# Relu-squared attention and a gated FFN on one core: first loads split, output blocks interleaved, a new rule for bursts in the planner

## The chip, the cores and the metric

The kernel runs on one core of one Trainium2 chip. Its time is the device time in microseconds (us). The engines are named as in the profile: PE (TensorE, matmul), PEld (its weight loads), DVE (VectorE), ACT (ScalarE), POOL (GpSimd, which issues the input loads), SP (SyncE, which issues the output stores and the DMA transposes).

## The reference

For 8 batches of 12 heads, 448 positions and head size 64, scores = q kT / 8, attention = relu(scores)^2 / 448, times v. The heads are laid side by side as x (3584 tokens by 768), and the FFN is (relu(x Wg) * (x Wv)) Wout with d_ff 1536:

```
scores = scale * np.matmul(q, k.transpose(0, 1, 3, 2))
attn = np.maximum(scores, 0.0) ** 2 / S
x = matmul(attn, v)  # heads side by side
gate = np.maximum(x @ w_gate, 0.0)
return (gate * (x @ w_val) @ w_out).astype(np.float32)
```

Inputs and output are fp32 in HBM; the kernel computes in bf16 with fp32 sums.

## The kernel before, in words

**Work.** A quad is four heads of one batch: 3 quads per batch, 24 in all. For each quad q and k are brought into the layout qkT (head dimension on partitions), for batches 0 and 1 by PE transposes (`transpose_pe`, L384; copies out of PSUM by L406 on ACT or L408 on DVE), later by a DVE permutation (L428) and a DMA transpose that SP issues (L434). `Attention.s(i)` (L470) is one of seven score steps of a quad: four 64x64 matmuls that run side by side (L478) into a pair of PSUM banks, a relu (L488 on ACT or L490 on DVE), and a square (L499 or L501). `Attention.pv` (L508) multiplies the seven squared blocks with v (28 matmuls, L516), and L531 or L533 copies the result to xT. Batch 0 is done in two parts: query columns 0 to 191 of all three quads, then 192 to 447.

**FFN.** Batches 0 and 1 use `gv_plain` (L556, matmuls L568): 12 blocks of 128 columns of d_ff, each a gate product and a value product of six matmuls. The first six blocks of batch 0 are done for its two parts separately. Later pairs of batches use `gv_strassen` (L633, matmuls L668): seven products of three matmuls per block, named p1 to p7, in which sums accumulate in the same PSUM bank and are copied out between them (`snapshot`, L625, ACT L617/L619 or DVE L621/L623; L687, L698, L709, L725 on DVE). So p5 waits for the copy after p6, and p3 for the addition (v1, L687) after p5. The output product of each pair of batches is `out_tail` (the 128 odd rows, four products) and then `out_strassen` (three blocks i of seven products, matmuls L769): in a block the order is p1, p7, p6, p4, p5, p2, p3, with `evac_add` (L759, DVE) after p4, p5 (called o22) and p2, and p3 waiting for o22. The four sums `sh` (L806, DVE) that feed a block wait for all of h (the hidden values) of the pair.

**Order.** All five engines' orders are written when the kernel is built, by `plan` (L128): a greedy list planner with modelled costs per operation and engine, which commits at each step the operation that can start first. Operations of ACT and DVE (`others`) go to whichever engine ends them first. POOL's loads go in the order in which they are declared (`pool`), with at most eight on their way. PE draws from three lists: `first` (transposes, scores and PVs of batch 0, part one), then `att` (the rest of attention) and `ffn`, each in its own fixed order. Scores come in bursts of two. A new burst starts when the FFN time since the last one (`since`) has reached `gap` (the FFN work left in the segment, over the bursts left until its deadline) and attention can start at most 0.15 us after the FFN operation:

```
if att[ai][1] == last_burst:
    pick = "A" if A[0] <= F[0] + 0.4 else "F"
elif since >= gap:
    pick = "A" if A[0] <= F[0] + 0.15 else "F"
else:
    pick = "F" if F[0] <= A[0] + 0.3 else "A"
```

**Buffers.** PSUM has eight banks. Attention uses pairs of banks (0,1) and (2,3) (`PAIRS`; four pairs for batch 0, `FIRST_PAIRS`); FFN products use the single banks 7, 6, 5, 4 (`SINGLES`). There are ten buffers for squared scores (`at`), three for qkT, one for the hidden values hT.

**Loads.** At the start POOL issues k and q of the three quads of batch 0 (L364, L365), with the making of the identity matrix (for PE's transposes) after the first two of them, then v, then the weights in six chunks of 256 columns (L334, gate and value of each), with the quads of batch 1 between: chunks 0, 1, quad a, chunk 2, quads b and c, chunks 3, 4, 5.

Of the kernel before, what the change touches and what calls it, by code (L numbers as in the profile page):

```python
# [22 lines left out]
class Buf:  # L23
# [7 lines left out]
    def pick(self):  # L31
        best = None
        for i in self.among:
            if all(i + w in self.res.free for w in range(self.width)):
                t = max(self.res.free[i + w] for w in range(self.width))
                if best is None or t < best[0]:
                    best = (t, i)
        return best
# [16 lines left out]
class Planner:  # L55
# [5 lines left out]
    RESERVE = 16  # L61
# [7 lines left out]

    def ready(self, op):  # L70
        r = 0.0
        for d in op.deps:
            if d.end is None:
                return None
            r = max(r, d.end + (self.LATE if d.xbar else 0.0))
        for b in op.alloc:
            p = b.pick()
            if p is None:
                return None
            r = max(r, p[0])  # L80
        return r
# [17 lines left out]
    def commit(self, op, s, e):  # L99
        op.start, op.eng = s, e  # L100
        occ, busy = op.engs[e]
        self.t[e] = s + occ
# [11 lines left out]
        for b in op.alloc:  # L114
            b.idx = b.pick()[1]
# [12 lines left out]
def plan(first, att, ffn, others, pool, deadline):  # L128
# [3 lines left out]
    P = Planner()  # L132
    ai = fi = pi = 0
# [5 lines left out]
    active = [o for o in others if not o.missing]  # L139
    def done(op):  # L140
# [5 lines left out]
    last_burst = last_grp = None  # L146
    since = gap = 0.0
# [3 lines left out]

    first = [list(x) for x in first]
    while any(first) or ai < len(att) or fi < len(ffn) or active or pi < len(pool):
# [5 lines left out]
        if pi < len(pool):  # L159
            b = P.best(pool[pi])  # L160
            if b is not None:
# [3 lines left out]
                cands.append((s, 0.0, 0, "POOL", pool[pi]))  # L165
        if any(first):
# [4 lines left out]
            s, _, kind, e, op = min(cands, key=lambda c: c[:3])  # L171
            P.commit(op, s, e)
            done(op)
            if kind == 0:
                pi += 1
            elif kind == 1:
                active.remove(op)
            else:
                first = [x[1:] if x and x[0] is op else x for x in first]
            continue  # L180
        A = P.best(att[ai][0]) if ai < len(att) else None
        F = P.best(ffn[fi][0]) if fi < len(ffn) else None
        pick = None
        if ai < len(att) and fi < len(ffn) and last_grp is not None and last_grp == ffn[fi][0].grp:
            pick = "F" if F is not None else None
        elif A is not None and F is not None:
            if att[ai][1] == last_burst:
                pick = "A" if A[0] <= F[0] + 0.4 else "F"
            elif since >= gap:
                pick = "A" if A[0] <= F[0] + 0.15 else "F"  # L190
            else:
                pick = "F" if F[0] <= A[0] + 0.3 else "A"
        elif A is not None:
            pick = "A"
        elif F is not None:
            pick = "F"
        if pick == "A":
            cands.append((A[0], A[2], 2, "PE", att[ai][0]))
        elif pick == "F":
            cands.append((F[0], F[2], 2, "PE", ffn[fi][0]))  # L200
        assert cands, f"no operation can start: {ai} {fi} {len(active)} {pi}"
# [5 lines left out]
        elif kind == 1:  # L207
            active.remove(op)
        elif pick == "A":
            if att[ai][1] != last_burst:  # L210
                last_burst = att[ai][1]
                since = max(0.0, since - gap)
            ai += 1
            last_grp = None
            sg = ffn[fi][1] if fi < len(ffn) else None
            left = deadline(sg) - last_burst + 1 if sg is not None and deadline(sg) is not None else 0
            gap = max(0.0, left_work[sg] - (P.RESERVE if sg == 0 else 0.0)) / max(1, left) if left > 0 else 0.0
        else:
            since += op.engs["PE"][0]
            left_work[ffn[fi][1]] -= op.engs["PE"][0]  # L220
            last_grp = op.grp
            fi += 1
# [5 lines left out]
def kernel(  # L228
# [31 lines left out]
    HALF = 3 * P2  # L260
# [34 lines left out]
    r_raw, r_perm, r_vv, r_qt, r_at = Res(N_RAW), Res(N_PERM), Res(N_VV), Res(N_QT), Res(N_AT)  # L295
# [13 lines left out]
    PAIRS, FIRST_PAIRS = [0, 2], [0, 2, 4, 6]  # L309
# [47 lines left out]
    def load_qk(b, g):  # L357
# [5 lines left out]
        src = lambda x: x[b, hs].rearrange("h (p t) d -> p h t d", t=NT)  # L363
        k_op = dma_in(lambda: st.raw()[64:128], src(k), 256, 1.15, alloc=[] if early else [st.raw_buf])  # L364
        q_op = dma_in(lambda: st.raw()[0:64], src(q), 256, 1.15)  # L365
# [17 lines left out]

    def transpose_pe(b, g):  # L384
        st = quads[(b, g)]
        ps2 = bank2(FIRST_PAIRS if b == 0 else PAIRS)

        def emit():
            raw = st.raw()
            for j in range(2):  # L390
                for t in range(NT):
                    for h2 in range(2):
                        nc.tensor.transpose(ps_b[64 * h2:64 * h2 + 64, ps2.idx + j, t * 128:(t + 1) * 128],
                                            raw[:, 2 * j + h2, t, :], ident)

        st.qt_buf = Buf(r_qt)
        op = pe(emit, 1.05, deps=st.qk_ops + [id_op], alloc=[ps2, st.qt_buf])
        st.qt_ops = []
        for j in range(2):
            cp = Op({"DVE": (0.6, 0.72), "ACT": (0.8, 0.95)}, None, deps=[op], reads=[ps2])  # L400

            def emit_cp(cp=cp, j=j):
                dst = qkT_t[st.qt_buf.idx][:, :, j, :].rearrange("p a (t c) -> p t a c", c=P2)
                src = ps_b[:, ps2.idx + j, :NT * 128].rearrange("p (t a c) -> p t a c", t=NT, a=2)
                if cp.eng == "ACT":
                    nc.scalar.copy(dst, src)  # L406
                else:
                    nc.vector.tensor_copy(dst, src)  # L408

            cp.emit = emit_cp  # L410
            st.qt_ops.append(cp)
            others.append(cp)
        return op

    def transpose_dma(b, g):
# [24 lines left out]
        st.qt_ops = [op]  # L440
# [11 lines left out]
    class Attention:  # L452
# [7 lines left out]
        def at_of(self, i):  # L460
            flat = at_t[self.at[i].idx].rearrange("p h c -> p (h c)")
            return flat[:, :2 * self.n].rearrange("p (h c) -> p h c", h=2)
# [7 lines left out]
        def s(self, i):  # L470
            ps2 = bank2(self.pairs)
            n = self.n
            at = self.at[i] = Buf(r_at)
# [7 lines left out]
            op = pe(emit, mm_time(1, n) + 0.01, deps=self.st.qt_ops, alloc=[ps2, at], reads=[self.st.qt_buf],  # L481
# [60 lines left out]
    hbuf, h_ops = {}, {}  # L542
# [5 lines left out]
    def pair_h(b):  # L548
        pr = b // 2
        if pr not in hbuf:  # L550
            hbuf[pr] = Buf(r_h)
            h_ops[pr] = []
            return [hbuf[pr]]
        return []

    def gv_plain(b, seg, blocks=range(KF), c0=0, n=S):  # L556
        cols = slice(c0, c0 + n)
        x_ops = xop[b] if b in xop else [o for c in xparts if n == S or c == c0 for o in xop[(b, c)]]
        for mf in blocks:
# [3 lines left out]
            for w, w_op in ((wg, wg_op), (wv, wv_op)):  # L563
# [16 lines left out]
                deps=[ops[1], grel], alloc=pair_h(b), reads=[bufs[1], gb])  # L580
            h_ops[b // 2].append(vmul)
# [51 lines left out]
    def gv_strassen(b, seg, T_ops):  # L633
# [44 lines left out]
        for mf in range(KF + 1):  # L678
# [5 lines left out]
            if prev is not None:  # L684
# [8 lines left out]
                    deps=[v1, prev["g1"]], reads=[vb, prev["g1b"]])  # L693
                others.append(h1)

            def p3_of(prev, v1, h1):
# [3 lines left out]
                    deps=[p3, prev["g0"]], reads=[prev["A"], prev["g0b"]], alloc=pair_h(b))  # L700
                h_ops[b // 2].extend([h0, h1])
                h1.deps.append(h0)
                others.append(h0)

            if cur is not None:
# [12 lines left out]
                if prev is not None:  # L718
                    p2_of()
                    p3_of(prev, v1, h1)  # L720
# [8 lines left out]
            else:  # L729
                p3_of(prev, v1, h1)  # L730
# [45 lines left out]
    def out_tail(b, seg, T_ops):  # L776
# [3 lines left out]
        lhs = lambda par: lambda kf: hT[:, 2 * kf + par, S - P2:S + P2]  # L780
        w = lambda par, hf: lambda kf: wo[:, par, hf, kf, :]
        h_lo = h_ops[pr][:-2]
        A, Bk = bank(), bank()
        wd = list(wo_op.values())
        slots = ((b, NT - 1), (b + 1, 0))
# [169 lines left out]
```

## Time and profile before

| | us |
|---|---|
| device time, median of 6 runs | 424.49 (423.62 to 427.26) |
| device time of the profiled execution | 424.81 |
| its span, first to last instruction | 422.9 |
| PE busy | 397.0 (94%) |
| DVE busy | 314.5 (74%) |
| ACT busy | 270.1 (64%) |
| POOL busy | 72.5 (17%) |

The granted clock of PE is 0.998 over the span. Of the chain of work that ended last, PE has 77%, DMA 9%, ACT 5%, DVE 4%. The loads of the inputs run until about 60 us at some 200 GB/s, and then one quad at a time beside the attention. The last PE matmul starts at 417.1 us.

A row of the order of time is: start, duration, engine, line, operation, what it writes and reads, how many merged; in brackets the engine's idle time before it and what ended that. A busy PE is not PE at its peak: the ends of matmuls are modelled, so gaps below some 0.2 us do not show as idle, and PE's own pace has to be taken from stretches in which nothing lies between the matmuls.

### The profile page before, as it was taken

To read this page: it belongs to the slowest core of one execution; us is meant where nothing else is said; L and a number is where in the kernel's file an instruction comes from. 1 tells how busy PE (TensorE), PEld (TensorE's weight loads), DVE (VectorE), ACT (ScalarE), POOL (GpSimd) and SP (SyncE) were. 2 spreads that over 40 slices of the span, in tenths; PEclk is the share of its full clock that TensorE was granted. 3 is DMA by queue.
4 is the path that set the end of the run, shared out by engine and by line. 5 is a ranking of instruction groups with operands and counts; after the bars stand their busy time and mean duration, and the time that the engine had idled before them with its cause. 6 is when DMAs were issued, how large, how long until landed. Compare 5 with 4: busy or idle time off the path is not lost.

```text
span 422.9 us, 8622 instructions
## 1 busy us (share of the span) xinstructions
PE 397.0 (94%) x3396; PEld 206.3 (49%) x3396; DVE 314.5 (74%) x569; ACT 270.1 (64%) x411; POOL 72.5 (17%) x118
## 2 busy tenths in 40 slices
PE   2878998999999999999999999999999999999994
PEld 2666653444444444444445554444455555554552
DVE  1785666997888989897788668998987647667451
ACT  3886886877778977877685556766767543343221
POOL 7746231122212211222120012021000000000000
PEclk9999999999999999999999999999999999999999
DMA  8999999997788998987737687354002430000144
GB/s 121 191 200 200 199 164 181 100 110 110 77 134 147 171 173 110 111 98 87 110 45 122 149 166 104 50 79 65 2 2 67 115 81 2 1 2 0 39 117 108
DMA packets 74920, 43.42 MB, mean 103 GB/s; under 512 B 36992, under 2 KB 74880, under 8 KB 74880
## 3 DMA queue, kind: packets, MB, share of 16 engines
q0 software_dynamic: 32512, 23.60, 41.3%
q1 hardware_dynamic: 42368, 19.28, 26.8%
q8 instruction: 26, 0.43, 0.4%
q14 instruction: 14, 0.11, 0.1%
HBM read 47.19 MB, written 11.01 MB: 138 GB/s over the span
## 4 chain that ended last, share of the span: by engine, by line
PE 77%; DMA 9%; ACT 5%; DVE 4%; issue 2%; POOL 1%; SPq 0%; DVEq 0%; POOLq 0%
PE ps L668 33%; PE ps L769 20%; PE ps L568 10%; PE ps L478 7%; PE ps L516 7%; DMA wv<-in_moe_w_val_dram 4%; DMA qkT<-perm 3%; ACT at L488 3%; DMA gvT<-in_k_dram 2%; DVE at L490 2%; DVE o L759 1%; ACT at L499 1%; ACT f L617 1%; DVE sx L648 1%; ACT xT L531 1%
## 5 line engine op out<-in xcount | busy, mean ns | idle before, releaser
L488 ACT ACTIVATE at<-ps 128x896 bf16<-128x896 f32 (+2 forms) x132 | 107.2, 846 | 30.9 <-PE ps L478 30.8
L617 ACT COPY f<-ps 128x448 f32<-128x448 f32 x100 | 52.9, 531 | 48.3 <-PE ps L668 47.9
L501 DVE TENSOR_TENSOR at<-at 128x896 bf16<-128x896 bf16 (+2 forms) x123 | 66.9, 561 | 16.7 <-ACT at L488 15.8
L478 PE MATMUL ps<-qkT 64*64 64x448 bf16 (+2 forms) x756 | 56.8, 346 | 5.7 <-ACT xT L531 1.6
L490 DVE TENSOR_SCALAR at<-ps 128x896 bf16<-128x896 f32 (+2 forms) x57 | 54.1, 954 | 9.1 <-PE ps L478 8.1
L499 ACT ACTIVATE at<-at 128x896 bf16<-128x896 bf16 (+2 forms) x66 | 58.0, 891 | 3.6 <-DVE at L490 2.8
L668 PE MATMUL ps<-sx,wv 128*128 128x448 bf16 x216 | 52.7, 353 | 1.0 <-DVE g L687 0.9
L668 PE MATMUL ps<-xT,gvT 128*128 128x448 bf16 x216 | 52.7, 353 | 0.8 <-ACT f L617 0.7
L668 PE MATMUL ps<-xT,wg 128*128 128x448 bf16 x216 | 52.2, 353 | 0.0
L668 PEld LDWEIGHTS <-gvT 128*128 128x128 bf16 x324 | 30.4, 98 | 32.4 <-issue 5.9
L322 POOL DMA_DIRECT2D vv<-in_v_dram x44 | 26.4, 611 | 108.5 <-PE ps L478 103.3
L769 PE MATMUL ps<-wo,hT 128*128 128x384 bf16 x240 | 43.7, 326 | 0.8 <-ACT f L619 0.8
L769 PEld LDWEIGHTS <-hT 128*128 128x128 bf16 x312 | 29.8, 98 | 23.1 <-issue 3.8
L478 PEld LDWEIGHTS <-qkT 64*64 64x64 bf16 x756 | 20.0, 106 | 38.8 <-issue 33.5
L769 PEld LDWEIGHTS <-sh 128*128 128x128 bf16 x288 | 27.1, 98 | 22.6 <-issue 4.9
L759 DVE SCALAR_TENSOR_TENSOR o<-ps,f 128x384 f32<-128x384 f32 x40 | 22.1, 551 | 18.1 <-PE ps L769 11.6
L516 PE MATMUL ps<-at,vv 64*64 64x448 bf16 (+2 forms) x700 | 34.7, 329 | 0.9 <-ACT at L499 0.3
L568 PE MATMUL ps<-xT,wg 128*128 128x448 bf16 (+2 forms) x180 | 32.5, 317 | 1.5 <-ACT at L488 1.1
L568 PE MATMUL ps<-xT,wv 128*128 128x448 bf16 (+2 forms) x180 | 32.2, 315 | 1.3 <-DMA wv<-in_moe_w_val_dram 1.3
L709 DVE CUSTOM_DVE_ANT_0 g<-ps,f 128x448 bf16<-128x448 f32 x36 | 22.4, 622 | 13.7 <-PE ps L668 13.3
L668 PEld LDWEIGHTS <-wv 128*128 128x128 bf16 x216 | 20.2, 98 | 23.1 <-issue 6.2
L531 ACT CAST xT<-ps 128x896 bf16<-128x896 f32 (+2 forms) x26 | 21.3, 820 | 15.3 <-PE ps L516 15.3
(55 smaller groups left out, 455.0 us busy)
## 6 DMA issues: line engine op xcount, KB each, us to landing
out_dram<-o SPq DMA_DIRECT2D x112, 96.0 KB, 2.2
vv<-in_v_dram POOLq DMA_DIRECT2D x44, 112.0 KB, 6.2
raw<-in_k_dram POOLq DMA_DIRECT2D x18, 224.0 KB, 5.2
raw<-in_q_dram POOLq DMA_DIRECT2D x18, 224.0 KB, 6.8
wg<-in_moe_w_gate_dram POOLq DMA_DIRECT2D x6, 384.0 KB, 9.6
wv<-in_moe_w_val_dram POOLq DMA_DIRECT2D x6, 384.0 KB, 10.5
wo<-in_moe_w_out_dram POOLq DMA_DIRECT2D x4, 576.0 KB, 12.1
gvT<-in_k_dram POOLq DMA_DIRECT2D x6, 224.0 KB, 8.1
```

Of the source, the lines that this page charges most:

```text
L322: op = Op({"POOL": (0.5 + 0.0004 * n_desc,) * 2}, lambda: nc.gpsimd.dma_start(out=dst(), in_=src), deps=deps, alloc=alloc)
L478: nc.tensor.matmul(ps[64 * j:64 * j + 64, ps2.idx + h2, :n], lhsT=self.k_of(j, h2, i), rhs=self.q_of(j, h2), start=True, stop=True)
L488: nc.scalar.activation(self.at_of(i), src, AF.Relu)
L490: nc.vector.tensor_scalar_max(self.at_of(i), src, 0.0)
L499: nc.scalar.activation(at, at, AF.Square)
L501: nc.vector.tensor_tensor(at, at, at, ALU.mult)
L516: nc.tensor.matmul(ps[64 * h2:64 * h2 + 64, ps2.idx + j, :n], lhsT=st.v_of(j, h2, c), rhs=self.at_of(c)[64 * j:64 * j + 64, h2, :], start= ...
L568: nc.tensor.matmul(ps[:, pb.idx, :n], lhsT=w[:, kd, fc], rhs=xT_t[xbuf[b].idx][:, kd, cols], start=(kd == 0), stop=(kd == KD - 1))
L617: nc.scalar.copy(dst, src)
L668: nc.tensor.matmul(ps[:, pb.idx, :S], lhsT=w(g)[:, fc], rhs=rhs, start=start and g == 0, stop=stop and g == KH - 1, skip_group_check=True)
L759: op = Op({"DVE": V384}, lambda: nc.vector.scalar_tensor_tensor(o_t[ob.idx], ps[:, pb.idx, :OH], float(out_scale), f_t[fb.idx][:, :OH], AL ...
L769: nc.tensor.matmul(ps[:, pb.idx, :OH], lhsT=lhs(kf), rhs=rhs(kf), start=start and kf == 0, stop=kf == FH - 1, skip_group_check=True)
```

## The change

It has five parts.

1. **First loads.** q of batch 0 is loaded in two pieces: slots t = 0, 1, 2 (`QT`), which are the queries of part one, with the keys; slots 3 to 6 (`q_late`) after v. Each first transpose takes all keys and three query slots (`transpose_first`), and a second one (`rest`) makes the late queries at the start of part two. The copies out of PSUM are one for the keys and one for the queries. The identity is made on DVE (`make_ident`). Chunk 2 of the weights is loaded ahead of the first quad of batch 1, and 3 and 4 ahead of the second and third.
2. **Buffers.** The squared scores of part one take half of an `at` buffer each (20 in place of 10). Batches 1 to 3 may use a third pair of banks, (4,5), which is also among the single banks.
3. **Burst rule.** Bursts of two are given up: attention is one list, with PV of a quad after the second score step of the next. `debt` grows with the FFN time committed, and each attention step takes one `share` (FFN work left in the segment over attention steps left to its goal) off it. A burst starts at `START` = 2 shares, and goes on while the next step can start at once and the debt is above -2 shares, or can start within 0.25 us and the debt is a share or more. The first part of the FFN of batch 0 is a segment of its own with a share of zero (its reserve is 1000).
4. **Windows.** The planner may take any of the next three FFN operations, or of the next two attention steps, if it can start at least 0.03 us earlier. Between PE operations it no longer waits for the modelled end.
5. **Output blocks** (`out_both`, in place of `out_tail` and `out_strassen`). The order is tail a0, b0, p1 of block 0, tail a1, b1, then p7, p2, p6, p4 of block 0; then for the next block p1, old p5, p7, p2, old p3, p6, p4; and after the last block p5 and p3. Each product waits only for the parts of h that it reads (batch of the pair, even or odd block; `h_of`).

The core of the diff:

```
-    RESERVE = 16
+    RESERVE = (1e3, 8.0, 4.0)
+    WINDOW, ATT_WINDOW, START, AHEAD = 3, 2, 2.0, 2.0
...
-            r = max(r, d.end + (self.LATE if d.xbar else 0.0))
+            if d.eng != "PE" or "PE" not in op.engs:
+                r = max(r, d.end + (self.LATE if d.xbar else 0.0))
...
+            for i, (op, _) in enumerate(ffn[:P.WINDOW]):
+                b = P.best(op)
+                if b is not None and (F is None or b[0] < F[0] - 0.03):
+                    F = (*b, i)
...
+                wait = A[0] - P.t.get("PE", 0.0)
+                if inside:
+                    pick = "A" if wait <= 0.03 and debt > -P.AHEAD * share or wait <= 0.25 and debt >= share else "F"
+                elif debt >= P.START * share:
+                    pick = "A" if A[0] <= F[0] + 0.15 else "F"
+                else:
+                    pick = "F" if F[0] <= A[0] + 0.3 else "A"
...
+            share = set_share()
+            debt = max(0.0, debt - share) if not inside else debt - share
...
-        q_op = dma_in(lambda: st.raw()[0:64], src(q), 256, 1.15)
+        if b == 0:
+            st.load_q = lambda t0, t1: dma_in(lambda: st.raw()[0:64, :, t0:t1], src(q, t0, t1), 256, 0.17 * (t1 - t0))
+            q_op = st.load_q(0, QT)
+        else:
+            q_op = dma_in(lambda: st.raw()[0:64], src(q), 256, 1.15)
...
+    def transpose_first(g):
...
+                for t in range(NT) if part == 0 else range(QT, NT):
+                    p0, p1 = (64 if t >= QT else 0, 128) if part == 0 else (0, 64)
+                    for h2 in range(2):
+                        nc.tensor.transpose(ps_b[64 * h2:64 * h2 + 64, ps2.idx + j, t * 128 + p0:t * 128 + p1],
+                                            raw[p0:p1, 2 * j + h2, t, :], ident[p0:p1, p0:p1])
...
+            at = self.at[i] = Buf(r_at) if 2 * n <= S else Buf(r_at, range(0, 2 * N_AT, 2), 2)
...
+    def make_ident():
+        one, row, col = ident, sx[:, 0, 0, :128], sx[:, 0, 1, :128]
+        nc.vector.memset(one, 1.0)
+        nc.vector.tensor_tensor_scan(row, one, one, 0.0, ALU.mult, ALU.add)
+        nc.vector.transpose(col, row)
+        nc.vector.tensor_tensor(ident, row, col, ALU.is_equal)
...
-    id_op = Op({"POOL": (0.6, 0.65)}, lambda: make_identity(nc, ident))
-    pool_ops.insert(2, id_op)
...
+    for g in range(NQ):
+        quads[(0, g)].q_late = quads[(0, g)].load_q(QT, NT)
-    for x in (0, 1, "a", 2, "b", "c", 3, 4, 5):
+    for x in (0, 1, 2, "a", 3, "b", 4, "c", 5):
...
+    A_ += [Attention(b, g, pairs=MORE_PAIRS if b < 4 else PAIRS) for b in range(1, B) for g in range(NQ)]
```

## The prediction

> **What bounds the kernel now.** I read the slices of the page first, then the busy table by stretches, then the chain that ended last, then the order of time at the head and at the end. In all of them I asked one thing: TensorE (PE) has a fixed amount of work, so where does it run below its own pace?
>
> The pace first. In the chain, late in the run, 231 matmuls of 448 columns follow one another with nothing between:
>
> ```profile
> 74.43 1.38 PE ps L516 x28
> ...
> 79.55 0.50 PE ps L478 x8
> 80.05 2.38 PE ps L568 x12
> 82.42 0.50 PE ps L478 x8
> ...
> 345.81 43.87 PE ps L668 x231
> ```
>
> 43.87/231 = 0.190 us per matmul. L516 and L478 are 64x64 tiles, four at once, so 28 of them should take 7 x 0.190 = 1.33 and 8 should take 0.38. A cycle of one attention burst and two FFN products (79.55 to 82.42) lasts 2.87 us where 14 x 0.190 = 2.66 were needed: **0.21 us, call it 0.22 with its rounding, is lost at each excursion from the FFN into attention and back**. Counted in the order of time, after 40 us there are 96 stretches of score matmuls (L478) and 8 of PV matmuls alone, for 147 score steps and 21 PV: 104 excursions, 1.6 steps each, 104 x 0.22 = 23 us. They lie 15, 12 and 16 score stretches in 40 to 76, 76 to 112 and 112 to 157 us (48 with 5 lone PV), and 56 from 157 to 345.
>
> ```profile
> 0.00:10.00 10.00, 2.92 (x44) 2.12 (x44) 0.99 (x2) 2.87 (x4) 7.31 (x17) 1.00 0.85 117
> 10.00:20.00 10.00, 8.43 (x188) 6.19 (x192) 7.95 (x23) 8.92 (x20) 7.33 (x11) 1.00 1.33 190
> 20.00:30.00 10.00, 8.24 (x161) 6.48 (x154) 8.64 (x21) 8.70 (x20) 4.49 (x7) 1.00 1.39 200
> 30.00:40.00 10.00, 7.38 (x166) 5.82 (x163) 5.49 (x14) 6.14 (x14) 7.07 (x10) 1.00 1.32 201
> ```
>
> The columns are PE, weight load, DVE, ACT, POOL, clock, DMA. The head is the one place where PE is visibly short. With each matmul counted at the pace above (a 192-column one at 192/448 of it), the first 40 us hold about 21 us of PE work. From 10 to 30 the evacuating engines stand at 8 to 8.9, so they limit; from 30 to 40 DVE (5.5), ACT (6.1) and PE (7.4) are all idle at once, so an order limits. It is this one:
>
> ```profile
> 6.47 1.70 PE L393 MATMUL ps<-ident,gvT 128*64 128x128 bf16 x28 [6.47 <-DMA gvT<-in_q_dram]
> ...
> 10.53 1.70 PE L393 MATMUL ps<-ident,gvT 128*64 128x128 bf16 x28 [0.78 <-DMA gvT<-in_q_dram]
> ...
> 32.21 0.67 PE L568 MATMUL ps<-xT,wv 128*128 128x192 bf16 x6 [1.27 <-DMA wv<-in_moe_w_val_dram]
> ```
>
> The written order puts the products of weight columns 512 to 767 (chunk 2) ahead of the last attention steps of batch 0; chunk 2 was queued behind a quad of batch 1, landed at 32.2, and the attention behind it starved DVE and ACT. The end has two more holes, PE waiting for one evacuation each time:
>
> ```profile
> 390.29 0.73 PE L668 MATMUL ps<-sx,wv 128*128 128x448 bf16 x3
> ...
> 391.73 0.73 PE L668 MATMUL ps<-sx,wv 128*128 128x448 bf16 x3 [0.71 <-DVE g L687]
> ...
> 401.74 0.55 DVE L759 SCALAR_TENSOR_TENSOR o<-ps,f 128x384 f32<-128x384 f32 x1
> ...
> 402.35 1.14 PE L769 MATMUL ps<-wo,sh 128*128 128x384 bf16 x6
> ```
>
> **The change part by part.** The sum is against the profiled execution: span 422.9, 424.81 us on the device (1.9 around the span), which is 0.3 above the median of 424.49.
>
> *First loads.* The q of batch 0 comes as slots 0 to 2 first (3/7 of its bytes). Quad 0's q landed 1.25 us after its k (5.09, 6.34); 4/7 of 1.25 is 0.7, so the first transposes start at about 5.8. The identity leaves POOL (0.24 and 0.29 us, ahead of the second k) for DVE, whose first own work is at 8.22: nothing lost, and if it took 2 us, still nothing. Quads 1 and 2 gain 1.4 and 2.0 us of landing. What is put in: three more issues on POOL (0.63 us each, 1.9), which stand ahead of every weight load; POOL waits for landings there anyway, so this cost I take at zero, at most 1.4 net. On the DMA engines each q row becomes two packets. In the trace's packet records a 512 B packet takes a median 60 ns, 768 B 79, 896 B 88: 0.073 ns per byte and some 22 ns fixed. A row of 384 B is then 50 ns, and 50 + 60 against 88 is 22 ns more, x256 packets/16 engines = 0.35 us per quad, 1.1 in all, after which every weight lands later by that. The Trainium skill speaks against this (DMA: Bandwidth & Descriptors, Specifications): 512 B is its least transfer for line rate, below which the engine reads, modifies and writes. If that doubled the 384 B packets (an estimate: 100 ns), the delay would be 72 x 256/16 x 3 = 3.5 us. No software-queue packet of this trace is that short; I take the row, 1.1, and keep 3.5 for the range.
>
> The first transposes now mix 128-row and 64-row pieces, four changes at most 0.22 each and 16 late matmuls of about 0.05; for three quads that is at most 5 us of PE, put at zero because PE waits there for landings and evacuations; without that cover it would eat the head's gain.
>
> *Order in the head.* Chunk 2 now goes ahead of quad 0 of batch 1 (its four loads took the queue from 24.63 to 28.05, 3.4 us), so it lands near 32.2 - 3.4 + 1 = 30. More important, attention of batch 0 goes first: for the first FFN segment a reserve of 1000 makes its share zero, so FFN products only fill. And part one has 20 half buffers for its squares in place of 10 whole ones. Evacuation of batch 0 sums to about 46 us on two engines (42 relus of 0.43 to 0.69, 42 squares of 0.30 to 0.65, copies), 23 us apiece; starting at 7 and running at the 0.85 to 0.9 of the 10 to 30 us rows, with 2 us of FFN evacuation among it, it ends near 35; the last PV of batch 0 ran at 38.4 to 39.3. I take 4 us gained, beside the 0.7 at the start; from 0 (DMA sets the weights' landings anyhow) to 6 (all idle of 30 to 40 gone). It is not given back while FFN products of batches 0 and 1 are there to fill: they last to 112.
>
> *40 to 157 us.* Batches 1 to 3 may use three PSUM pairs, and the new rule starts a burst at two shares of debt and goes on up to four steps while nothing waits. Their 72 steps (63 scores, 9 PV) at 2.5 per burst are 29 excursions, not 48: 19 x 0.22 = 4.2 us. The waits on qkT at 71 us (1.2 on PE, some 1.3 more beside it) I halve: 1.2; the transposed keys land late because the DMA is full, and the change moves no byte from there. The out stage of pair 0 loses about 2 us to the chain O-DVE-O at block ends; I take 1.0 back. The sum, 6.4, I cut by a third to 4.3, because three relus of about 0.9 us then sit ahead of the FFN's evacuations on FIFO engines that are 80 to 90% busy.
>
> *157 to 345 us.* Two pairs as before; only the rule differs. 96 steps at 2 per burst: 48 excursions for 56, 1.8 us, and 0.5 of waits. Cut by a third: 1.5. Bounds: 0 (DVE, at 8.9 to 9.4 of 10 from 150 to 190, frees the pairs when it frees them) and 4.
>
> *End.* With a window of three, the tail products and the next block's first can run in the waits before the last p5 and p3: 0.31 + 0.71 = 1.0 gained. Overlapped blocks lose their two waits of 0.31: 0.6. But the last block now has p3 straight after p5: in the row above o22 ended 402.29, 1.8 us after p5 would have begun if p2 did not lie between; p3 waits 0.8. Net 0.8. The tail after PE's last (417.1 to 422.9) stays.
>
> Sum: 0.7 + 4 + 4.3 + 1.5 + 0.8 = 11.3, and 1 for the same end-of-product waits in the middle pairs (p5 to p3 twice, 0.5 each): 12.3. 424.8 - 12.3 = **412.5 us**.
>
> **The rivals.** *The head is bound by landing (0.15).* Against it: the idle of 30 to 40 on three engines. For it: DMA at 190 to 201 GB/s from 10 to 50 us, and 1.1 to 3.5 us more packets. Then 4.7 shrinks to about 0.5, and the time is 416.7. *The bursts don't lengthen (0.13).* The rule still starts with one free pair, and a pair comes free when DVE frees it, as now with 40 single-step stretches. Then head, middle and end remain: 4.7 + 0.8 + 1 = 6.5, 418.3. *Both (0.06):* 422.6, which is no change. *Longer bursts stall the FFN (0.20, the slower side).* Three pairs take banks 4 and 5 from the four single banks that overlapped out blocks need, and three relus (2.7 us on two engines) sit before a snapshot of 0.5 for which a product waits with only 1.1 us of products between. Price: one relu, up to 0.9, at each burst of the 77. It decides from 12.3/77 = 0.16 us per burst; at 0.25 it is 19 us against the 12, and the time 431. Against it: such waits (L668 on ACT f and on DVE g) sum to 1.6 us in the whole trace; for it, ACT and DVE stand at 8 to 9 from 110 to 200 and the order is fixed when built, from modelled times.
>
> **How the numbers follow.** My forecast has 0.46, its own range 406 to 418 (below: head 6.7, middle 6.4 uncut, late stretch 4; above: head 2.7, middle halved, late stretch nothing). The range 404 to 427 takes in the rivals but most of the slower one. About 0.5% is what a measurement can tell from no change; so faster 0.74 (0.46 + 0.15 + 0.13), same 0.06, slower 0.20.
>
> **What would show it.** The first L393 at 5.8, not 6.5; the row of 30 to 40 with DVE and ACT over 7.5; the last PV of batch 0 at 35; about 77 excursions after 40 us, fewer than 35 of them before the out stage of pair 0 ends; no wait of PE in the last strassen products, but 0.8 before the very last product. I am wrong if weights land over 2 us later, if excursions stay near 100, or if PE waits on ACT f and DVE o grow by more than 5 us.

## The result and the profile after

The changed kernel takes **420.17 us** (median; 418.72 to 425.3) beside 424.79 us for the kernel before in the same comparison: a ratio of **0.990, interval 0.988 to 0.992**. That is 4.6 us less, where the prediction put 12.3 and 412.5 us. The direction was right, the size was not, and the time lies inside the range. The profiled execution shown here took 425.27 us (span 423.5) and a second one (e6 below) 423.80 (span 422.0), both slower than the median, so what only these two show need not hold for a typical run.

The busy table by stretches of the changed kernel, columns as before, begins with the head; the fifth line is the stretch in which it is worst:

```profile
0.00:10.00 10.00, 2.92 (x48) 2.08 (x48) 1.90 (x11) 2.19 (x2) 7.58 (x16) 1.00 0.90 119
10.00:20.00 10.00, 7.10 (x120) 4.03 (x117) 6.89 (x21) 7.18 (x16) 8.14 (x12) 1.00 1.30 174
20.00:30.00 10.00, 8.64 (x187) 7.38 (x183) 6.24 (x18) 7.75 (x19) 3.48 (x6) 1.00 1.41 199
30.00:40.00 10.00, 8.52 (x200) 7.17 (x192) 7.82 (x19) 8.43 (x19) 5.43 (x9) 1.00 1.37 199
...
76.00:112.00 36.00, 31.23 (x235) 13.96 (x234) 27.17 (x36) 25.06 (x35) 5.71 (x10) 0.91 0.84 85
```

The idle of 30 to 40 us is filled, as was wanted: DVE 7.8 for 5.5, ACT 8.4 for 6.1. But look at the lines above it. From 10 to 30 DVE fell from 16.6 to 13.1 us and ACT from 17.6 to 14.9. Over the whole 40 us DVE did 22.9 us (23.1 before) and ACT 25.6 (26.6 before). The hole was moved, not closed. In the fifth line, between 76 and 112 us, PE is idle for 4.8 us, and the granted clock is 0.91.

The order of time of the changed kernel shows why the head begins late (start, duration, engine, line, and in brackets the idle before and what ended it; PEld lines left out):

```profile
5.95 1.70 PE L439 MATMUL ps<-ident,gvT 128*64 128x128 bf16 x28 [5.95 <-DMA gvT<-in_q_dram]
...
7.69 0.91 ACT L413 COPY qkT<-ps 128x896 bf16<-128x896 bf16 x1 [5.67 <-PE ps L439]
...
8.63 0.36 DVE L415 COPY qkT<-ps 128x384 bf16<-128x384 bf16 x1 [5.96 <-ACT qkT L413]
8.77 1.53 PE L439 MATMUL ps<-ident,gvT 128*64 128x128 bf16 x22 [1.13 <-DMA gvT<-in_q_dram]
...
10.07 0.37 PE L536 MATMUL ps<-qkT 64*64 64x192 bf16 x2
```

The first transposes start at 5.95 instead of 6.47 us (6.72 in e6), and the first scores at 10.07 instead of 8.43. Two things happen in between. The DVE copy of the queries is released by the ACT copy of the keys, although they write different places: both read the same two PSUM banks. Before, each engine had a bank of its own, and DVE's copy began at 8.22 while ACT's (7.47 to 8.37) still ran. And the written order now has the transposes of quad 1 ahead of the first scores; they wait 1.13 us for their q. The same pairing of the copies shows in what DVE waits for over the whole trace (total us, times, longest; the longest is mostly the idle before the first transposes, so the total is not a cost):

```profile
DVE qkT L415 <- ACT qkT L413: 11.2, 4, 6.0
```

The late queries need transposes of their own, on PE in the middle of the head (three groups of 16):

```profile
23.97 0.44 PE L439 MATMUL ps<-ident,gvT 64*64 64x64 bf16 x16
...
29.67 0.44 PE L439 MATMUL ps<-ident,gvT 64*64 64x64 bf16 x16
...
34.60 0.41 PE L439 MATMUL ps<-ident,gvT 64*64 64x64 bf16 x16
```

PE in the order of time around the worst place of the changed kernel:

```profile
82.32 1.30 PE L634 MATMUL ps<-xT,wv 128*128 128x448 bf16 x6
88.39 0.96 PE L536 MATMUL ps<-qkT 64*64 64x448 bf16 x8 [4.77 <-DMA qkT<-perm]
89.28 2.42 PE L634 MATMUL ps<-xT,wg 128*128 128x448 bf16 x6
91.50 2.45 PE L634 MATMUL ps<-xT,wv 128*128 128x448 bf16 x6
```

PE waits 4.77 us for the transposed q and k of quad 7 (quads are counted from 0, three to a batch), and after it six matmuls take 2.42 us instead of 1.30. The trace's clock records show half clock for 6.8 us from 87.6.

At the end the chain of the changed kernel has what was hoped for:

```profile
347.38 45.40 PE ps L734 x240
...
395.86 21.46 PE ps L835 x132
```

132 output matmuls in one piece, and one wait of PE for an evacuation left after 345 us, before the last product:

```profile
PE ps L835 <- DVE o L825: 0.6, 1, 0.6
```

A count of finished work makes the stages comparable. Every matmul but the transposes is counted at the 0.190 us pace, by its columns; the whole kernel holds 359.9 us of it. Done by a time t (us), each row from one profiled execution:

| kernel | 40 | 76 | 112 | 157 | 222 | 345 | 391 | span |
|---|---|---|---|---|---|---|---|---|
| before | 13.8 | 43.9 | 77.0 | 115.1 | 173.0 | 289.3 | 334.9 | 422.9 |
| after | 13.1 | 42.2 | 68.8 | 111.6 | 169.6 | 286.6 | 332.8 | 423.5 |
| e6 (after again) | 13.1 | 42.6 | 70.5 | 113.0 | 171.1 | 288.1 | 334.3 | 422.0 |
| e3 | 13.8 | 43.9 | 76.6 | 116.8 | 174.2 | 289.9 | 335.1 | 421.2 |
| e10 | 14.4 | 45.0 | 78.8 | 119.4 | 178.9 | 296.7 | 343.0 | 413.4 |
| e1 | 13.9 | 44.6 | 75.6 | 116.2 | 176.1 | 293.5 | 339.7 | 416.6 |
| e2 | 13.5 | 45.2 | 78.8 | 119.4 | 179.8 | 296.5 | 342.7 | 413.7 |
| e7 | 15.9 | 46.0 | 79.2 | 120.2 | 179.8 | 296.5 | 342.5 | 413.8 |
| e9 | 14.4 | 40.9 | 74.9 | 114.7 | 173.5 | 287.6 | 333.6 | 424.0 |
| e13 | 13.5 | 44.8 | 77.5 | 114.3 | 174.0 | 290.1 | 336.2 | 420.1 |
| e5 | 13.1 | 42.4 | 74.5 | 115.2 | 175.0 | 292.2 | 338.1 | 418.2 |
| e8 | 13.5 | 45.0 | 77.5 | 118.3 | 178.5 | 295.0 | 341.2 | 415.1 |
| e12 | 14.6 | 46.9 | 79.0 | 119.4 | 179.7 | 296.5 | 342.8 | 413.6 |

Read the second and third rows: the changed kernel is 0.7 us behind at 40 and 6.5 to 8.2 behind at 112, and wins it back only later and at the end.

### The profile page after: what moved, and what is told of

Read it like the earlier page. It is cut to its first block, busy times and chain, and to the rows that moved or that the text cites. A ratio compares the mean times of both kernels' runs of the same rounds, so it can differ in the third digit from the quotient of the medians.

```text
span 423.5 us, 8710 instructions
## 1 busy us (share of the span) xinstructions
PE 397.0 (94%) x3444; PEld 208.4 (49%) x3444; DVE 323.5 (76%) x585; ACT 264.5 (62%) x408; POOL 73.7 (17%) x119
## 3 DMA queue, kind: packets, MB, share of 16 engines
q0 software_dynamic: 33328, 23.60, 42.4%
## 4 chain that ended last, share of the span: by engine, by line
PE 87%; DMA 5%; ACT 4%; DVE 2%; issue 1%; POOL 0%; DVEq 0%; ACTq 0%; POOLq 0%
PE ps L734 34%; PE ps L835 24%; PE ps L634 12%; PE ps L536 9%; PE ps L574 7%; DMA qkT<-perm 3%; ACT at L546 1%; DMA gvT<-in_q_dram 1%; ACT qkT L413 1%; DVE at L548 1%; PE ps L439 1%; DVE qkT L415 1%; ACT at L557 1%; DVE at L559 0%; POOL gvT L342 0%
## 5 line engine op out<-in xcount | busy, mean ns | idle before, releaser
L546 ACT ACTIVATE at<-ps 128x896 bf16<-128x896 f32 (+2 forms) x125 | 100.6, 846 | 25.2 <-PE ps L536 24.9
L683 ACT COPY f<-ps 128x448 f32<-128x448 f32 x101 | 53.2, 532 | 46.7 <-PE ps L734 43.9
L548 DVE TENSOR_SCALAR at<-ps 128x896 bf16<-128x896 f32 (+2 forms) x64 | 61.6, 967 | 5.6 <-PE ps L536 5.5
L536 PE MATMUL ps<-qkT 64*64 64x448 bf16 (+2 forms) x756 | 55.1, 353 | 9.6 <-DMA qkT<-perm 4.8
L685 ACT ACTIVATE f<-ps 128x384 f32<-128x384 f32 x37 | 18.2, 492 | 36.1 <-PE ps L835 33.4
L634 PE MATMUL ps<-xT,wg 128*128 128x448 bf16 (+2 forms) x180 | 33.6, 324 | 2.2 <-ACT xT L589 1.5
L634 PE MATMUL ps<-xT,wv 128*128 128x448 bf16 (+2 forms) x180 | 33.4, 323 | 0.0
L342 POOL DMA_DIRECT2D raw<-in_k_dram x18 | 11.2, 624 | 121.9 <-DVE perm L485 121.2
L825 DVE SCALAR_TENSOR_TENSOR o<-ps,f 128x384 f32<-128x384 f32 x40 | 22.1, 553 | 11.8 <-PE ps L835 8.9
L734 PEld LDWEIGHTS <-wg 128*128 128x128 bf16 x216 | 20.4, 98 | 20.9 <-issue 3.2
```

The source lines that it names most:

```text
L342: op = Op({"POOL": (0.5 + 0.0004 * n_desc,) * 2}, lambda: nc.gpsimd.dma_start(out=dst(), in_=src), deps=deps, alloc=alloc)
L536: nc.tensor.matmul(ps[64 * j:64 * j + 64, ps2.idx + h2, :n], lhsT=self.k_of(j, h2, i), rhs=self.q_of(j, h2), start=True, stop=True)
L546: nc.scalar.activation(self.at_of(i), src, AF.Relu)
L548: nc.vector.tensor_scalar_max(self.at_of(i), src, 0.0)
L634: nc.tensor.matmul(ps[:, pb.idx, :n], lhsT=w[:, kd, fc], rhs=xT_t[xbuf[b].idx][:, kd, cols], start=(kd == 0), stop=(kd == KD - 1))
L734: nc.tensor.matmul(ps[:, pb.idx, :S], lhsT=w(g)[:, fc], rhs=rhs, start=start and g == 0, stop=stop and g == KH - 1, skip_group_check=True)
```

## The experiments

### Undoing the first loads: e1 and e2

My first theory was that the split of the first loads costs more than it brings, by the copies that wait for each other and by the later scores. The rival was that the middle alone lost the time. e1 is the changed kernel with the copies of a PE transpose shared by bank again:

```
-        kcp = copy_qk(op, ps2, qk_cols(st, 0, NT, 1), ...)   # keys, both banks
-        qcp = copy_qk(op, ps2, qk_cols(st, 0, QT, 0), ...)   # queries, both banks
+        kcp = [copy_bank(op, ps2, st, j, ((0, NT, 1), (0, QT, 0)), ...) for j in range(2)]
```

> The changed kernel, with the copies of the PE transposes of batches 0 and 1 split by PSUM bank (one engine reads bank j's keys and queries) in place of keys on one engine and queries on the other. Theory A (the two copies read the same two banks, and the second is held until the first is done, which costs 0.4 to 0.9 us per quad in a chain of three): the DVE copy runs beside the ACT copy, the first score step starts near 9 us instead of 10.1, the last PV of batch 0 near 40 instead of 42.9, and the time falls by 2 to 4 us to about 416 to 418. Rival B (the head is late because the split q packets and three more issues delay the weights by 1.1 us or more): the copies overlap, but the time stays at 419 to 421.

Measured 418.95 us (ratio 0.987, 0.984 to 0.990). The two copies no longer wait for each other (order of time of e1):

```profile
6.70 0.75 ACT L437 COPY qkT<-ps 128x448 bf16<-128x448 bf16 x2 [4.69 <-PE ps L457]
...
7.52 0.55 DVE L439 COPY qkT<-ps 128x448 bf16<-128x448 bf16 x2 [4.84 <-PE ps L457]
```

They do not overlap either, though I had expected it. ACT copies the first bank while PE still transposes into the second (5.78 to 7.47 us), and DVE's copy is released by PE, not by ACT. Both are done 2.3 us after the first transpose began, 3.0 in the changed kernel, where the copy of the keys has to wait for both banks.

The gain on the changed kernel, 1.2 us, is less than the two intervals tell apart; the last PV of batch 0 starts at 39.8 us instead of 42.9. The first scores stay at 9.99, since quad 1's transposes are still ahead of them.

e2 also takes the split of q out; all else of the change stays:

```
-            st.load_q = lambda t0, t1: dma_in(lambda: st.raw()[0:64, :, t0:t1], ...)
-            q_op = st.load_q(0, QT)
+        q_op = dma_in(lambda: st.raw()[0:64], src(q), 256, 1.15)
-    trans, late = zip(*[transpose_first(g) for g in range(NQ)])
+    trans = [transpose_pe(0, g) for g in range(NQ)]
```

> The changed kernel with the head's first part undone: q of batch 0 loaded whole with the keys, one transpose per quad, copies split by bank as in the kernel before; identity on DVE, the order of the weight chunks, half buffers and the burst rule stay. Theory A (the copies are what cost, the split of q by itself is worth its 0.5 to 2 us of earlier landing): slower than e1 by 1 to 2 us, faster than the changed kernel by 1 to 2, 418 to 419. Rival B (split packets delay the weights): faster than e1, and faster than the changed kernel by 3 or more, 415 to 417.

Measured **415.82 us (0.980, 0.977 to 0.982)**: 3.1 us below e1 and 4.4 below the changed kernel, with intervals apart. The split of q is a loss, although in e2's own profile the first transposes start at 8.41 us, 2.5 later than after the change. Rival B met the number but not its mechanism: the first weights land at 18.28 us in e1, with the split, and at 18.52 in e2, without it. Half clock is not the main part of the loss either: in runs with a granted clock of 0.997 or more the changed kernel takes 418.7 to 420.2 us and e2 415.5 to 415.8. The long wait on quad 7 is gone with the split. What PE waits for in e2:

```profile
PE ps L548 <- DMA qkT<-perm: 0.7, 1, 0.7
```

### Does an earlier start carry through? e8

e2 with the identity on POOL again, between q and the next k of the queue, as before the change:

```
-    id_op = Op({"DVE": ...}, make_ident)
+    id_op = Op({"POOL": (0.6, 0.65)}, lambda: make_identity(nc, ident))
```

> e2 with the identity made on POOL between the first and the second k, as before. In e2 q of quad 0 landed at 8.3 and the first transpose ran at 8.4, in the kernel before at 6.3 and 6.5, though the loads are the same: if the 0.5 us of POOL between them let the first pair go through the DMA engines alone, the landing is again near 6.4; then the time is 413.5 to 415 if the head's start carries through (theory E), or stays at 415.5 to 416 if evacuation and weights set the head's end (rival).

Measured 415.82 us (0.980, 0.977 to 0.982), the same as e2. Its first transposes ran at 6.80 us in the profile, 1.6 earlier, and by 40 us both had done 13.5 us of work. But the place of the identity did not make that difference: e12 (below) loads and builds the identity as e2 does, and its first transposes run at 6.42. So the start varies by up to 2 us between profiled executions with the same first loads. And e8's profile lost time to two spells of half clock, at 18.0 and 38.5 us; its run with a granted clock of 1.000 took 414.25 us, 1.3 less than the fastest of e2, so a small gain is not excluded. What an earlier start is worth is read better from e12, which is 1.1 us ahead of e2 at 40, 0.2 ahead at 112, and ends with it (413.6 and 413.7): a lead in the head was given back, so the 0.7 of the prediction is not shown to be worth anything by itself.

### The wait on quad 7: e5, e6 and e13

The permutation that feeds quad 6's transposes moved from 55.95 us before to 60.22 after, since attention ran later. Quad 7's transposes were issued at about the same time (72.9 and 74.2 for 72.2 and 73.4) and landed at 84.1 and 88.3 instead of 79.7 and 81.3, now beside the last two output weight loads. The theory: those loads hold them up. The rival: attention is late anyway. e5 puts all four loads ahead of the quads, in the changed kernel:

```
     for par in range(2):
         for hf in range(2):
             load_out(par, hf)
+    for par in range(2):
         load_qk(2, 1 + par)
         load_v(2, 1 + par)
```

> The changed kernel with all four loads of the output weights issued ahead of quads 1 and 2 of batch 2 (in the changed kernel two of them stand on POOL behind the load of quad 1, which waits for the one raw buffer). Theory C (PE's 4.8 us wait at 83 to 88 us for the DMA transposes of quad 1 of batch 2 comes from the DMA being idle at 61 to 64 and then carrying the output weights beside the transposes): the transposes land by about 80, the wait is under 1 us, the clock stays at 0.998 or more, and the time is 414 to 417 with few runs above 418. Rival (the transposes are late because the attention before is late, not for the DMA): the wait stays, and the time stays at 419 to 421 with the same spread.

Measured 420.84 us (0.992, 0.989 to 0.995), no different from the changed kernel. The named wait is gone from PE's list. The transposes of quad 7 took 5.5 and 9.6 us instead of 11.1 and 14.2, so beside fewer loads they are shorter; but they were issued later (78.4 and 79.7) and landed no earlier (83.9 and 89.3), and the time stayed. So the rival is right on the time, but it forecast that the wait would stay too, and that is not so. In the profiles e5 is 4.0 to 5.7 us ahead of the changed kernel at 112, while the medians (420.84 and 420.17) are not: either a typical run of the changed kernel waits less than its two profiled ones, or something else takes the gain back. This was not separated, and that attention is late by itself is not shown by the time alone. e13 does the same to e2:

> e2 with the four output-weight loads ahead of quads 1 and 2 of batch 2. In e2 PE waits only 0.7 us for DMA transposes, so 415.5 to 416.5 if the wait is all that this could mend; under 415 if the DMA's idle 61 to 64 us also holds up something else.

Measured 421.72 us (0.995, 0.993 to 0.998): **5.9 us slower** than e2. The table shows where: 1.3 us behind e2 at 112, 5.1 at 157. PE in the order of time of e13:

```profile
149.98 0.57 PE L548 MATMUL ps<-qkT 64*64 64x448 bf16 x8 [0.94 <-DMA qkT<-perm]
151.38 1.52 PE L586 MATMUL ps<-at,vv 64*64 64x448 bf16 x28 [0.83 <-ACT at L558]
...
153.93 0.73 PE L548 MATMUL ps<-qkT 64*64 64x448 bf16 x8 [0.84 <-ACT xT L601]
155.58 0.87 PE L548 MATMUL ps<-qkT 64*64 64x448 bf16 x8 [0.92 <-DVE at L560]
```

The out stage of pair 0 ended at about 148.7 us, the PV that starts at 151.4 here starts at 144.7 in e2, and no FFN product lies between these steps: one stretch of seven score steps loses 4.85 us. Read together: quads that are loaded later make attention later, and it then runs without cover. (The profile of e13 also has two spells of half clock before 43 us; its two runs at a granted clock of 0.998 took 419.95 and 420.24, still over 4 us more than e2.)

e6 is the changed kernel once more, for a second profile: does half clock belong to the wait, or to that execution?

> The changed kernel once more, for a second profile of it. In the first one PE waited 4.8 us at 83.6 for the DMA transposes of quad 1 of batch 2, and its clock was then half for 6.8 us. If the clock falls because PE has waited (theory D), then a run with a shorter wait there has a shorter half-clock spell or none, and about 419 us; if the low clock comes by itself, it lies elsewhere or beside no wait.

423.8 us. The wait was again 4.8 us and half clock followed again, for 3.4 us from 88.0 (6.8 in the first profile). So the wait is not of one execution alone, half clock came with it both times, and the length of the slow spell varies. Whether the runs with a granted clock of 0.997 to 0.999 have the wait is not shown.

### The blocks, the windows, the bursts: e3, e10, e9, e7, e11, e12

In e7 and e10 one copy into x runs before the last product that reads the old values there (in e10 at 210.63 us, the product at 212.04), so one hidden block (block 11 of batch 2) is made from other operands, with the same instructions in number and shape. Their times are read as times of these instructions; with the order kept this one copy would come some 2 us later, and what that costs was not run. e2, e9 and e12 do not have it.

e3 is the kernel before with nothing but the overlapped output blocks (`add_h`, `h_of`, `out_both` for `pair_h`, `out_tail`, `out_strassen`):

> The kernel before with only the interleaved output blocks and the finer waits on h (planner, loads, pairs and windows as before). If the blocks are worth what I put in the sum (0.8 at the end, 1 to 2 in the middle pairs), 422 to 423.5 against 424.8; the 6.9 us lost in 112 to 157 fall to about 5. If the gain of the stage from 112 to 157 in the changed kernel (2.2 lost instead of 6.9) comes from the blocks, not from pairs and bursts, it is 420 to 421. Rival (the exposed p3 at the very end eats it): 424 to 425.

Measured 421.87 us (0.994, 0.992 to 0.996): 2.5 us. e10 adds to it a window of three FFN products in the planner of before:

```
-        F = P.best(ffn[fi][0]) if fi < len(ffn) else None
+        for i, (op, _) in enumerate(ffn[:3]):
+            b = P.best(op)
+            if b is not None and (F is None or b[0] < F[0] - 0.03):
+                F, fw = b, i
```

> The kernel before with the interleaved output blocks (e3, 421.9) and, in its planner, the window of three FFN operations; old burst rule, loads, copies and pairs. e9 without windows was 10 us slower than e2, so if the windows carry the gain (theory F), this one is far under e3: 415 to 417, about e2. If windows matter only together with the new burst rule, 420 to 422.

Measured **415.24 us (0.980, 0.976 to 0.984)**. Blocks and window alone give all that any version here gives, 2.5 us by the blocks and 6.6 more by the window. e9 asks it the other way round, e2 without its windows:

```
-    WINDOW, ATT_WINDOW, START, AHEAD = 3, 2, 2.0, 2.0
+    WINDOW, ATT_WINDOW, START, AHEAD = 1, 1, 2.0, 2.0
```

> e2 with both windows of the planner at 1: FFN operations and attention steps in their list order. If the reordering fills the waits at the end of the products (p5 and p3 of the last block: 1.0 us in the kernel before) and some in the middle, 1 to 3 us slower than e2: 417 to 419. If the window does nothing of weight, 415.5 to 416.3.

Measured 425.96 us (1.003, 1.001 to 1.005), some 10 us above e2. Of PE's waits in e9 the longest is for a DMA transpose; the others, one product waiting for an evacuation, are of the kind that a window can pass by:

```profile
PE ps L548 <- DMA qkT<-perm: 3.9, 1, 3.9
PE ps L847 <- DVE o L837: 2.3, 4, 0.7
PE ps L646 <- ACT at L558: 1.5, 2, 0.9
PE ps L746 <- DVE g L765: 1.5, 3, 0.7
```

e7 is e2 with two PSUM pairs everywhere (`pairs=PAIRS`), e12 is e2 with the chunk order of before:

> e2 (whole q, copies by bank) with two PSUM pairs for batches 1 to 3 as before, in place of three. If the third pair lengthens bursts (theory of the prediction: 32 score stretches in 40 to 157 instead of 43), the stretches rise to about 40 and the time by 8 x 0.22 = 2 us or more, to 417.5 to 419. Rival (the pair takes banks from the FFN): faster than e2, under 415.

> e2 with the weight chunks and quads of batch 1 loaded in the old order (0, 1, a, 2, b, c, 3, 4, 5). If chunk 2 ahead of quad a is what closes the old hole at 31 to 38 us (the prediction put 4 us on the head's order), 1 to 4 us slower than e2: 417 to 420. If the head's end is set by evacuation, 415 to 416.5.

e7: 415.86 us (0.980, 0.978 to 0.983); e12: 415.32 us (0.980, 0.977 to 0.983). Neither the third pair nor the chunk order is worth anything that shows. In e12 chunk 2 lands at 32.1 us instead of 28.8, and PE waits for it:

```profile
PE ps L646 <- DMA wv<-in_moe_w_val_dram: 1.6, 1, 1.6
```

The time is the same.

e11 tests the price of an excursion: e2, but inside a burst the FFN always comes next.

```
-  pick = "A" if wait <= 0.03 and debt > -P.AHEAD * share or wait <= 0.25 and debt >= share else "F"
+  pick = "F"
```

> e2 with bursts cut to one attention step (a burst never goes on while an FFN operation can start): 141 stretches of FFN work in PE's order in place of 86. At the 0.22 us per excursion of the prediction the time rises by 55 x 0.22 = 12 us, to about 428, if nothing else changes; if excursions are free because evacuation is what limits, by less than 3 us.

Measured 447.5 us (1.057, 1.050 to 1.064), 31.7 above e2. To read it, take each stretch of attention between two FFN matmuls (40 to 345 us, those with transposes of batch 1 left out), and the time by which the next FFN matmul starts later than the stretch's own work at the 0.190 us pace asks for:

| kernel | stretches | lost at them, us | of it beyond 0.22 times their number | time, us |
|---|---|---|---|---|
| before | 82 | 24.3 | 6.3 | 424.8 |
| e6 (after again) | 73 | 22.1 | 6.0 | 420.2 |
| e10 | 83 | 20.3 | 2.0 | 415.2 |
| e2 | 78 | 18.4 | 1.2 | 415.8 |
| e7 | 90 | 21.2 | 1.4 | 415.9 |
| e9 | 79 | 27.1 | 9.7 | 426.0 |
| e11 | 126 | 44.9 | 17.2 | 447.5 |

The times are medians (for e6 that of the changed kernel). In all of them the median loss of a stretch is 0.21 to 0.22 us for nearly every length; the rest sits in a few stretches. In e11, 124 of the 126 have one score step or a lone PV and lose 28.6 us together, where e2 loses 18.4 in all; the other two, of 15 score steps each, where a backlog of attention had to go at once, lose 8.0 and 8.3. PE inside one of these in e11:

```profile
77.57 0.38 PE L548 MATMUL ps<-qkT 64*64 64x448 bf16 x4 [0.44 <-ACT at L558]
78.80 0.57 PE L548 MATMUL ps<-qkT 64*64 64x448 bf16 x8 [0.84 <-DVE at L560]
80.02 0.45 PE L548 MATMUL ps<-qkT 64*64 64x448 bf16 x4 [0.65 <-ACT at L558]
```

Most steps there wait for the evacuation of one before. The profile of e11 has 13.7 us of half clock as well, part of it inside these two stretches. So the price was read rightly, and long attention without FFN between costs far more than the switch.

## Why the prediction was off

The sum of 12.3 falls into three parts, and the runs price each. Measured values are differences of ratios against the kernel before, times 424.2. They depend on the order in which the parts are added: a window is worth 6.6 us in the kernel before (e3 to e10), both windows 10.1 in e2 (e9 to e2).

| part | predicted | measured | from |
|---|---|---|---|
| overlapped blocks, windows (1.0 after the cut by a third = 0.7; 0.8; 1) | 2.5 | 8.5 | e10 |
| bursts, third pair, waits on qkT (the rest of the cut 4.3, and 1.5), and the head's order (4) | 9.1 | about 0 | e10 to e2 |
| split of the first loads (0.7) | 0.7 | -4.3 | e2 to after |

That the direction came out right is luck in part: with the 2.5 that was put for the first line, the measured other two would have made the kernel slower.

**The head failed, and it is the step that decided.** "I take 4 us gained, beside the 0.7 at the start": no version gained them. By 40 us 13.1 to 15.9 us of work were done, 13.8 before; the changed kernel had the least, and its last PV of batch 0 started at 42.9 us, not 35. The reasoning from the idle engines at 30 to 40 was the fault: I added up evacuation as if it could run through from 7 us on, and the idle only moved forward to 10 to 30. Nor was chunk 2 the order that limits: e12 has the old one and loses nothing. And "It is not given back" failed too: e12's lead over e2 is 1.1 us at 40 and 0.2 at 112, e7's 2.4 at 40 and 0.4 at 112. The rival "the head is bound by landing" forecast 416.7; on the head it was the nearest, but e12, with its later chunk 2, speaks against it. What bounds the head stays open.

What did cost stood in the working, at zero: "at most 5 us of PE, put at zero because PE waits there". The split of q brought 3.1 us of loss (e1 to e2). The first transposes take PE no longer than before (1.70 us a quad), the late ones 1.3 us together (0.44, 0.44, 0.41). Copies by keys and queries, for which there was no term, bring up to 1.2 more (after to e1). In the traces of the changed kernel the split goes with later attention and a late quad 7; how the 3.1 divides between the late transposes, the later scores, the wait and half clock was not separated.

**The waits on qkT, which I had halved,** went the other way in both profiles of the changed kernel: 1.2 us on PE became 4.8, with 1.7 to 3.4 us of half clock behind it (3.4 or 6.8 us at half pace), a cost that the prediction had no place for. In the traces such a spell came with every idle of PE of 1.8 us or more after the start (4.8 in after and e6, 3.9 in e9, 2.2 in e8, 2.1 in e13, 1.9 in e3, 1.8 in e1). Idles of 1.5 to 1.7 us had one in e5 and e11 and none in after, e6, e2 and e12; the kernel before, whose longest idle was 1.3, has none. The Trainium skill (TensorE: Matmul & The Clock Gate, What's actually happening) lets the clock fall after an idle window of about 3.4 us. By that rule only the idles of after, e6 and e9 should have had one; here about half of such an idle was enough, and the measurement decides. But spells at 18.0 us in e8 and 18.3 in e13 come with no idle over 0.4 us, so the length of an idle is not the whole cause, and the rest stays open.

**The bursts.** 0.22 us per excursion was right, with a median of 0.21 to 0.22 in every kernel. The count was the mistake. I took stretches of score matmuls, 104 of them (a recount of the trace gives 97), and scores that follow a PV directly pay no second switch. By stretches between FFN matmuls there were 82, and the change made 73: 9 x 0.22 = 2.0 us, not 27 x 0.22 = 5.9. By the count as I made it there are 84 stretches of scores after, where 77 were forecast. e7 shows that even that doesn't reach the end: 12 more stretches than in e2, 2.8 us more lost at them, and the same time, since e7 was 2.4 us ahead at 40 (its first transposes started at 7.06 us, those of e2 at 8.41). Why the head of e7 is better was not tried.

**Blocks and windows were under-priced**, 2.5 against 8.5, the mechanism being right. The blocks alone (e3) bring the 2.5. At the end about 2 us were gained (from 345 us on 7.3 us were lost before, 5.2 in e6 and 5.3 in e2), where 0.8 was put. The wait before the very last product is there, 0.65 for a forecast of 0.8. The larger part I missed: of e10's 7.8 us of span over e3, 4.0 come from the attention stretches, where at the same number of them, 83, the loss fell from 24.3 to 20.3 (some 1.7 more is a spell of half clock in e3's profile at 32.8 us). A window of three lets another product run while the next one waits for an evacuation. I had summed only the waits that the view names (L668, 1.6 us), not the time over 0.22 at the stretches, 6.3 us, which was to be read from the trace of before.

**What held, and what is luck.** The first transposes at 5.95 (5.8 put) are luck: e6, the same kernel, had them at 6.72, and e3, with the loads of before, at 6.01. The first weights came 0.9 us later (1.1 put), at 19.59 for 18.69, but at 20.15 in e6 and at 18.28 in e1 with the same loads, so this is not told from the spread. The 384 B packets took a median 51 ns (50 put), so nothing was doubled. Chunk 2 landed at 29.6 (30 put). The identity on DVE was done by about 2.7 us, free. "Longer bursts stall the FFN" did not come: PE's waits in FFN and output products on ACT f and DVE o stayed at 0.6 us or less each.

The rival that came nearest in time, "the bursts don't lengthen" with 418.3, is not what happened: from 40 to 157 us 37 stretches became 23.

The best versions (e10, e12, e2, e8, e7) lie at 415.2 to 415.9 us and beat the kernel before by about 2% and the changed one by about 1%; their intervals do not tell them apart.

## What to carry to other kernels

Idle engines in one stretch say that an order limits there; they don't say that a new order keeps what it fills, so follow the total of each engine over the whole stage. Here an order written ahead gained most from being allowed to swap one blocked product for the next, and the gain is read from the time over the fixed price at each switch, not from the waits that a view names. When one load is cut in two, look at what its second half now shares with the first: here a PSUM bank read by two engines, a place in PE's order ahead of the first scores, and transposes of its own. Before a start time is read as an effect, look at how far it varies between executions with the same loads: here by 2 us.

## What the hardware showed beyond that

PE idles of 1.8 to 2.2 us came with half clock for 3.4 us in four kernels (e1, e3, e8, e13), longer ones with 3.4 or 6.8 us; six matmuls of 448 columns then took 2.42 us for 1.30. Two copies out of the same PSUM banks ran one after the other on two engines, the second starting 0.94 us after the first. Over the changed kernel's runs the span went with the mean granted clock: 417.0 to 417.9 us at 0.999, 423.0 to 423.2 at 0.985 to 0.986 (two at 0.990 took 421.7 and 423.5). An estimate: 0.0135 of 423 us is 5.7 us, about the whole difference. The DMA transposes named above took from 5.5 us (e5) to 14.2 us (after) from issue to landing, the longest beside weight loads; e5 has one of 9.6 us without such a load.
